# A router input transposed by DMA and sine arguments summed in PSUM, in a kernel of a long convolution and a gated MLP

## The chip, the cores and the metric

The kernel runs on one core of one Trainium2 chip. Its time is the device time of one execution in microseconds (us). Five engines work side by side: TensorE (PE in the profile; its weight loads are PEld), VectorE (DVE), ScalarE (ACT), GpSimd (POOL) and SyncE (SP, which here only issues DMAs). Every engine executes its own list of instructions strictly in order, and lists wait for each other by semaphores.

## The reference

The input `x` has 2048 tokens of 512 channels. Two results are mixed by a gate per token.

```
g = sigmoid((x * gate_w).sum(-1))
# a: a state space layer, as a long causal convolution over the tokens
dt = exp(log_dt);  P[d,n,l] = exp(dt*(A_re + 1j*A_im)*l)           # 512 channels, 128 states, 2048 lags
K  = einsum("dn,dnl,dn->dl", Cc, P, dt*Bc).real                    # one filter per channel
a  = causal convolution of x with K (by FFT in the reference) + x * Dskip
# b: a gated MLP for the two tokens with the largest score, added to x
r = x @ w_r;  idx = top 2 of r
b = x;  b[idx] += sigmoid(r[idx]) * ((silu(x[idx] @ w_gate) * (x[idx] @ w_up)) @ w_down)
out = g * a + (1 - g) * b
```

Both `g` and `r` need, for each token, a product of the 512 channels with a vector. On TensorE that takes `x` with the channels on the partitions, the transpose of how `x` lies in memory.

## The kernel before

**Filters.** `P` is a product of exponentials and of sines and cosines of angles that grow with the lag. A lag is split into a coarse and a fine part: table 1 (`tab1`) holds the complex exponentials for the coarse lags, table 2 (`tab2`) for the fine ones, already multiplied by `C` and `B`. Each is made twice, for the two halves h = 0 and 1 of the channels. `kgen(h)` multiplies the tables on TensorE (L920) and sorts the filter into rows with small selecting matmuls (L933 to L949); `kspec(h)` turns it into its spectrum with the constant matrices `c_ksp` in the tiles KP (L975).

**Angles.** `B16` holds dt times A_im in units of 1/65536 of a turn, rounded to within one turn, in f32. For a group of up to four multiples, `trig` (L652) scales `B16` by each multiple into an int32 tile (`SCL`, ACT or DVE, L477), takes the Sin of the low 16 bits (L665), adds a quarter turn to the whole group (L667) and takes the Sin again for the cosine (L669). Table 1 uses three such groups for each half (four, four and two multiples, and the rest by doubling); table 2 uses two.

**Convolution.** `forward(blk)` transforms the two blocks of 1024 tokens with the matrices `c_fwd` in the tiles F (L896, groups of four matmuls), its results are evicted into `X` (L901), and four DMAs from GpSimd accumulate halves of it (L906). `products(h)` multiplies spectra on DVE, `inverse(h)` transforms back on TensorE (L1057), and the result is gated and stored.

**Routing.** `routing` (L759) makes the transposed input XT with 64 TensorE transposes of 128x128 in eight groups (L766), each evicted from PSUM by one copy of 128x1024 (L769, helper `EV`, L467). The matmuls of L781 give the two scores of each token. A chain of small DVE operations finds the two best tokens (four turns over TensorE, L800). Then `gat` (L828) gathers the two tokens, the MLP's first matmuls follow (L849, with the loads WG and WU of `w_gate` and `w_up`), its last ones (L863, here called dn, with the loads WD0 and WD1), a transpose of the result (L870), and a scaling into the row tile ZB on DVE (L873, called zby below). ZB also holds the row Dskip, loaded by a DMA of its own (zbd, L580), and zby waits for that load. An indirect DMA from GpSimd (L874) then adds the two rows to `out`, where two DMAs, dx0 and dx1 (L879), have copied the input before; `reload` (L883) reads it back into U.

**Order.** The order of all instructions on all engines, including the DMA queues, is written out in the text `ORDER`, which engine does an eviction or a scaling in `SECOND`, and which PSUM bank or place a temporary tile has in `PLACES`. SP therefore issues its DMAs in a fixed order as well, and a DMA whose wait isn't met holds up those behind it. WD lies where XT lay, so its loads wait for L781; the four tiles KP0 to KP3 lie where F lay, so their loads wait for the last forward matmuls that read each F.

Of the kernel before, what the change touches and what calls it, by code (L numbers as in the profile page):

```python
# [10 lines left out]
F32 = mybir.dt.float32  # L11
I32 = mybir.dt.int32
I16 = mybir.dt.int16
# [340 lines left out]
def small_mats():  # L354
# [17 lines left out]
    "00k00500201601501l00000100300700d00h00i00400900600800u00g00e00c00j00f00n00l00m08e00o00p00q00s00r00t01g01d01e01h00x00y00z01c01801704003x04104801a01b03z"  # L372
    "04a03y01003v02502604900w00v01x01v01101208g04b01w01r01z04201y02002302402102701t05g01u04504301s02202804c01304604402902a02j02k05h03w02l02m02n01402o06k06j"
    "04d05i02p04e04705m05j02q02r05k05n01q04f02s03401o01p02b01j01m01i01902c01n01f02t06s02u03702v06r04i02w02x02y03802z06p03004j03103204l03303904k03c04g04m03d"
    "04h03i06l03a03504n06m08f04o03g03b06q06n06o04p03j04q05o04r03h02d04u04s03m06x06y04t06z07002e01k04w07107204y03n04v08i06t08j04z04x06u07300a03l07403k03o00b"
    "03p05007607505p08l05405305q06v06w05l07807706703q06605108v07907a08k05r05u05t05207c08m03r08s06808n08t03s03603t07d07b08u05507i07h07g07f07e07l07k06906a05v"
    "07j05905a05605b05c05x08w08h06b08x05d05708z08o05e05w05y08y08p09009t09v07m07p07n07o07q08q09o08r09107r09309n07s07t09207v02g09407u09p09w09509602h09709807z"
    "07y09q09u08107w09r09s0a10a20a308207x09x09y06c06d06005z0a40a50a60a80a70aa0a906e09z08c0a00ac0ab0ad0ae06g06f06108a06208d06308009a09905806h08308409b06402f"
    "08509e08603e09g03f0af08708b0ag0ai09c0aq0ah05s03u05f06506i09d0am09i09f0ar0b00b209j0880b10as0an0ak0aj0b30al0at0b70b80b90b40b50b60ax0ay0au0av09h09k0ap0ao"
    "09l09m0az0ba0be02i0c50890cd0bd0bb0bg0bh0aw0c60cc0c70c30c20c10bc0bk0bj0c00bi0bf0bl0dk0bm0bn0bp0bo0bq0dl0dh0bt0bu0br0bs0by0di0ce0c80bv0bw0cf0bx0d30d40cg"  # L380
    "0ct0c90c40ch0co0ca0dd0dg0bz0cv0cu0df0de0d50dj0ci0cb0cw0d00et0cj0dn0d60cq0cx0cp0d10d20do0dt0cy0cz0cl0eu0ck0d70du0da0dr0dp0dm0dq0d80dx0cr0d90e80db0dc0cm"
    "0cn0f30f40dv0ey0ez0dw0cs0ds0e40e70ea0ev0ew0e90ef0e30eb0ed0eh0el0ex0fs0f00fv0f50f10e50fo0e60fu0fr0fn0em0f70f60f20ec0eg0en0ee0ej0ft0fw0fx0fz0f80eo0g00g5"
    "0ek0ei0f90gh0fq0fp0fy0g30gi0fa0fb0fc0fd0g10ge0gd0g60gj0g70gl0dy0gf0gg0gk0gn0g80fe0gm0go0gq0g20g40dz0gp0ff0fg0fi0gr0fh0fj0h00gv0fm0fl0gw0gx0gy0fk0es0gs"
    "0gt0gu0er0ep0eq0e00gb0ga0gc0e20g90h10e10h90gz0ha0h40h50h60h20h70hb0h30h80hc"
)
SECOND = (
    "000000000000000000000000000000000000100000000000000000000000000000101010100010100000100100000000000000000000000000100010000000000000000000000010010001"
    "000110010100001010010010011010000000000000000000000000000000000000000000000000000000001010010010100000100000000000000000000000000000000000000000000000"
    "000001000001010000000100000110100000100100000000101000000010000010000000000000000000000000000000000000000000000000000000000000000000000000000000000000"
    "000000000000000000000000000000000000000000000000000000000000000000000000000000000000000000000000000000000000000000000000000000000000000000000000000000"  # L390
    "0000000000010011000100000"
)
PLACES = (
    "2406154064740000000020660011001266446040110064604014001100111016606022026424242200101026264262451016541026000171234265"
)
KB = 1024


def bass_gated_mix__ssm_conv_s4__moe_arch_mod__prompt_kernel(nc, A_u, A_A_re, A_A_im, A_B_re, A_B_im, A_C_re, A_C_im, A_log_dt, A_Dskip,
# [20 lines left out]
    kp_c = const(kspec_mats(), "c_ksp")  # L420

    with ExitStack() as es:
# [76 lines left out]
        KP = [B("kp%d" % i, oF + 4 * i * KB, 4 * KB) for i in range(NU)]  # L499
        X = B("x", oX, 32 * KB)  # L500
# [7 lines left out]
        TMP = [B("tmp%d" % i, oTI[0] + (8 + 2 * i) * KB, 2 * KB, F32) for i in range(3)]  # L508
        CM1 = B("cm1", oTI[1], 4 * KB, F32); CM2 = B("cm2", oTI[1] + 4 * KB, 4 * KB, F32)
# [70 lines left out]
        DQ([(ZB(64, 1, 0, (1, D)), dr(A_Dskip, 0, (D, 1), (1, D)))], [], [(ZB, "d")], 1024)  # L580
        DQ([(WG(0, 128, 0, (NF, 4), (1, NF)), dr(B_w_gate, 0, (NF, 128), (128 * NF, 4), (1, NF)))], [], [WG], 1835008)
# [39 lines left out]
        STT(f512(B16), f512(tb_), c16, f512(TMP[2]), ALU.mult, ALU.subtract, [tb_, TMP[2]], [B16])  # L621
        c2 = lambda b, c=0: b(0, 128, c, (D, 2), (1, D))
# [29 lines left out]
        def trig(h, angs, ts, wide, tag, nn=None):  # L652
# [17 lines left out]
            return s  # L670
        def tab1(h, ts):
# [87 lines left out]
        def routing():  # L759
            for q in range(8):  # L760
                bb = misc(True)
                def tr(h, q=q, bb=bb):
                    last = None
                    for t_ in range(2):
                        for db in range(4):
                            last = h.transpose(bb(0, 128, db * 256 + t_ * 128, (1, 128)), U(0, 128, (2 * q + t_) * D + db * 128, (1, 128)), IDN(0, (1, 128)))  # L766
                    return last
                P.op(PE, tr, uk(2 * q, 2 * q + 1) + [CBI], [bb], cost=0.455)
                EV(XT[0](0, 128, q * 256, (2 * L, 2), (L, 2), (1, 256)), bb(0, 128, 0, (512, 2), (256, 2), (1, 256)), [bb], [(XT[i], q) for i in range(4)])  # L769
# [383 lines left out]
```

## Time and profile before

The runs of the kernel before took 153.70, 153.71 and 154.03 us, with a median of 153.71 us. The profiled execution took 153.72 us; its span, from the first to the last instruction, was 151.9 us, so 1.8 us lie outside the span.

| | busy us | share of the span | instructions |
|---|---|---|---|
| PE (matmuls) | 129.7 | 85% | 1605 |
| PEld (weight loads) | 96.4 | 63% | 1613 |
| DVE | 138.2 | 91% | 199 |
| ACT | 131.1 | 86% | 218 |
| POOL | 24.8 | 16% | 17 |

A window of the profile gives, for a stretch of the span, the busy time and the number of instructions of each engine, the clock granted to TensorE (1.00 is full), the busy share of the 16 DMA engines and the rate. A row of a group gives the line, the engine, the operation, the shapes and the count, then the busy time of all and the mean of one, then the idle time before them and what ended it. A mean of one on DVE and ACT is from start to end; back to back, the next one starts some 0.1 us before that end, so five copies of 0.69 us each take 3.0 us together.

### The profile page before, as it was taken

How to read it: one execution, taken by the hardware profiler on the slowest of the kernel's cores; microseconds unless marked ns; L12 is line 12 of the kernel's file. 1: busy time of each engine (PE TensorE's matmuls, PEld its weight loads, DVE VectorE, ACT ScalarE, POOL GpSimd, SP SyncE). 2: the span in 40 equal slices, each digit the busy share in tenths (PEclk: the TensorE clock that was granted, in tenths of full speed). 3: DMA queues.
4: the chain of work that ended last, by engine and by line, in shares of the span. 5: the costliest groups of instructions: out<-in, count | busy, mean ns of one | idle time of the engine just before them, and what ended most of it. 6: DMA issues, size and time to landing. Idle time of an engine off the chain costs nothing.

```text
span 151.9 us, 3786 instructions
## 1 busy us (share of the span) xinstructions
PE 129.7 (85%) x1605; PEld 96.4 (63%) x1613; DVE 138.2 (91%) x199; ACT 131.1 (86%) x218; POOL 24.8 (16%) x17
## 2 busy tenths in 40 slices
PE   0974787467989986979996999997999999999990
PEld 0944542464354336973454787995888867888880
DVE  0499999999999999999999974999999999999961
ACT  3599999999999999999999569397599999999731
POOL 3000001000122999910055000001000000000000
PEclk9999999955699999999997799999999999999999
DMA  5999999939908604000389997006800001014154
GB/s 136 344 293 388 414 403 404 350 108 330 365 2 119 162 0 138 4 5 0 92 231 254 275 275 118 6 4 203 356 0 2 4 2 35 0 54 123 35 173 138
DMA packets 14546, 24.09 MB, mean 159 GB/s; under 512 B 1175, under 2 KB 10146, under 8 KB 14370
## 3 DMA queue, kind: packets, MB, share of 16 engines
q1 hardware_dynamic: 11410, 21.11, 40.8%
q0 software_dynamic: 2144, 2.10, 9.0%
q10 hardware_dynamic: 976, 0.66, 1.6%
q8 instruction: 12, 0.20, 0.5%
q14 instruction: 4, 0.03, 0.1%
HBM read 19.66 MB, written 4.20 MB: 157 GB/s over the span
## 4 chain that ended last, share of the span: by engine, by line
PE 53%; DVE 28%; ACT 8%; DMA 6%; issue 3%; SPq 0%; ACTq 0%
PE ps L1057 18%; DVE AR L452 18%; PE ps L975 13%; PE ps L920 11%; DMA AR<-c_ksp 4%; DVE AR L467 3%; ACT AR L463 3%; PE ps L896 2%; PE ps L1010 2%; DVE AR L477 2%; ACT AR L467 2%; ACT AR L667 2%; DMA AR<-c_bf 2%; DVE AR L456 1%; PE ps L933 1%
## 5 line engine op out<-in xcount | busy, mean ns | idle before, releaser
L452 DVE TENSOR_TENSOR AR<-AR 128x1024 bf16<-128x1024 bf16 (+8 forms) x129 | 115.6, 952 | 7.2 <-DMA AR<-c_bf 3.8
L467 ACT ACTIVATE AR<-ps 128x1024 bf16<-128x1024 f32 (+10 forms) x45 | 35.0, 807 | 9.1 <-PE ps L975 4.7
L896 PE MATMUL ps<-AR 128*128 128x512 bf16 x122 | 31.0, 405 | 3.2 <-ACT AR L901 1.5
L1057 PE MATMUL ps<-AR 128*128 128x256 bf16 x256 | 29.5, 273 | 0.0
L1057 PEld LDWEIGHTS ps<-AR 128*128 128x128 bf16 x256 | 25.0, 98 | 3.1
L896 PEld LDWEIGHTS ps<-AR 128*128 128x128 bf16 x128 | 12.5, 104 | 18.9 <-issue 3.6
L975 PE MATMUL ps<-AR 128*128 128x256 bf16 x160 | 20.8, 288 | 1.3 <-DMA AR<-c_ksp 1.3
L975 PEld LDWEIGHTS ps<-AR 128*128 128x128 bf16 x160 | 16.4, 103 | 5.3 <-DMA AR<-c_ksp 1.6
L920 PE MATMUL ps<-AR 128*128 128x84 bf16 (+1 forms) x512 | 17.9, 196 | 1.7 <-DVE AR L452 1.7
L920 PEld LDWEIGHTS ps<-AR 128*128 128x128 bf16 x512 | 17.8, 96 | 2.2 <-ACT AR L463 2.2
L463 ACT ACTIVATE AR<-AR 128x1024 bf16<-128x1024 int16 (+5 forms) x24 | 18.5, 773 | 0.5 <-DVE AR L477 0.3
L463 ACT ACTIVATE ps<-AR 128x256 f32<-128x256 bf16 (+1 forms) x36 | 18.0, 549 | 0.1
L874 POOL DMA_INDIRECT out_dram<-AR x1 | 16.2, 16210 | 2.8 <-ACT AR L477 2.8
L901 ACT ACTIVATE AR<-ps 128x1024 bf16<-128x1024 f32 x16 | 15.9, 1015 | 0.0
L1068 ACT ACTIVATE AR<-ps,AR 128x256 bf16<-128x256 f32 x28 | 11.4, 482 | 4.3 <-PE ps L1057 3.4
L477 ACT ACTIVATE AR<-AR 128x256 int32<-128x256 f32 (+2 forms) x28 | 13.8, 518 | 0.0
L463 ACT ACTIVATE AR<-ps 128x512 bf16<-128x512 f32 (+1 forms) x18 | 11.9, 757 | 2.0 <-PE ps L597 2.0
L906 POOL DMA_DIRECT2D AR<-AR x4 | 5.3, 1464 | 17.6 <-ACT AR L901 16.0
L667 ACT ACTIVATE AR<-AR 128x1024 int32<-128x1024 int32 (+1 forms) x9 | 7.8, 867 | 0.1
L766 PE MATMUL ps<-AR 128*128 128x128 bf16 x64 | 4.6, 220 | 3.2 <-DVE AR L452 1.4
L477 DVE TENSOR_SCALAR AR<-AR 128x256 int32<-128x256 f32 (+2 forms) x20 | 6.5, 336 | 0.0
L766 PEld LDWEIGHTS ps<-AR 128*128 128x128 bf16 x64 | 3.6, 98 | 4.3 <-DVE AR L467 2.0
(67 smaller groups left out, 91.3 us busy)
## 6 DMA issues: line engine op xcount, KB each, us to landing
AR<-c_ksp SPq DMA_DIRECT2D x5, 512.0 KB, 3.9
AR<-in_A_u_dram SPq DMA_DIRECT2D x4, 512.0 KB, 5.5
AR<-c_fwd SPq DMA_DIRECT2D x4, 512.0 KB, 7.9
AR<-AR POOLq DMA_DIRECT2D x4, 512.0 KB, 12.9
AR<-out_dram SPq DMA_DIRECT2D x4, 512.0 KB, 10.1
AR<-c_inv SPq DMA_DIRECT2D x1, 2048.0 KB, 8.8
AR<-in_B_w_up_dram SPq DMA_DIRECT2D x1, 1792.0 KB, 12.0
AR<-in_B_w_gate_dram SPq DMA_DIRECT2D x1, 1792.0 KB, 16.1
```

Of the source, the lines that this page charges most:

```text
L452: return P.op(DVE, lambda h: h.tensor_tensor(out=o, in0=a, in1=b, op=op), rd, wr, cost=cst or tt_cost(o, a, b), **k)
L463: return P.op(ACT, lambda h: h.activation(out=o, in_=a, func=func, scale=scale, bias=bias), rd, wr, cost=0.185 + nel(o) * 0.833e-3 + (0.09 ...
L467: return P.op((ACT, DVE), (lambda h: h.activation(out=o, in_=a, func=ACTF.Copy), lambda h: h.tensor_copy(o, a)), rd, wr, cost=(0.185 + n * ...
L477: return P.op((ACT, DVE), (lambda h: h.activation(out=o, in_=a, func=ACTF.Copy, scale=c), lambda h: h.tensor_scalar(out=o, in0=a, scalar1= ...
L667: P.op((DVE, ACT), (lambda hh: hh.tensor_scalar(out=w, in0=w, scalar1=16384.0, scalar2=None, op0=ALU.add), lambda hh: hh.activation(out=w, ...
L874: P.op(POOL, lambda h: h.indirect_dma_start(dr(out, 0, (D, L), (1, D)), bass.IndirectOffsetOnAxis(ap=IDX(0, 2, 0, (1, 1)), axis=0), ZB(0, ...
L896: last = h.matmul(pb(0, 128, part * 512, (1, 512)), F[ft](0, 128, ((par * 4 + st) * 2 + part) * 128, (1, 128)), U(0, 128, (blk * 8 + st * ...
L901: P.op((ACT, DVE), (lambda hh, o=o, i_=i_, sc=sc: hh.activation(out=o, in_=i_, func=ACTF.Copy, scale=sc), lambda hh, o=o, i_=i_, sc=sc: hh ...
L920: last = hh.matmul(pb(0, 128, g // 6 * 512 + g % 6 * W4 + o, (1, n)), TP[h][1 - i // 2](0, 128, (b0 + g) * 128, (1, 128)), r[i](0, 128, (b ...
L975: last = hh.matmul(pb(0, 128, n * 256, (1, 256)), KP[u](0, 128, tau * 128, (1, 128)), KC[h](0, 128, jg * 256, (1, 256)), start=(k == 0 and ...
L1057: r = hh.matmul(pb(0, 128, e * 256, (1, 256)), G(0, 128, ((par * 2 + part) * 4 + ft) * 512 + (2 * t2 + e) * 128, (1, 128)), X(0, 128, blk ...
L1068: r = hh.activation(out=U(0, 128, tb * D + h * HC, (1, HC)), in_=pb(0, 128, e * 256, (1, HC)), func=ACTF.Copy, scale=SG(0, 128, 64 + tb, ( ...
```

## The change

The change has three parts.

- **Router input.** The eight groups of transposes and their eight evictions are gone. Four DMAs on SP's queue load the transposed input straight from memory, one for each 128 channels, all 2048 tokens, with `transpose=True`. The columns of XT are now in the order of the tokens, so L781's matmuls read them with a step of 2. `X` and all else of the routing are as before.
- **Angles of table 1.** From A_im and dt, six operations (five of them on 128x512 elements) make a value with few bits, split in two bf16 parts, PA[0] and PA[1]. For each group of table 1, `angles` takes the place of `trig`: TensorE multiplies the parts with a constant matrix `c_ang` (tile AN, a DMA of 164352 bytes) that holds the multiples, and sums them in PSUM on top of a large constant, so that the low 16 bits are the angle; ACT takes the Sin straight from PSUM; a matmul with a constant adds a quarter turn; ACT takes the Sin again. Table 2 keeps `trig`.
- **Order.** `ORDER`, `SECOND` and `PLACES` are new. Among others, SP issues XT1, XT0, XT3 and XT2 among the first loads; the loads of `c_bf`'s second part (cbo) and of zbd come after dx1 and before dx0; KP4 and two of the accumulating DMAs come later. `tab1(1)` is built ahead of the last load of KP instead of after it, which changes only its numbering.

```
+def angle_mats():   # 128 x 642: for each group the multiples, then 1.5 * 2**23 and 16384
...
+        AN = B("an", oF + 16 * KB, 2 * 642)
+        PA = [B("pa%d" % i, oF + 16 * KB + 1536 + i * KB, 1 * KB) for i in range(2)]
...
+        DQ([(AN(0, 128, 0, (1, 642)), an_c[:, :])], [], [AN], 164352)
...
+        for db in range(4):
+            P.op(SP, lambda h, db=db: [h.dma_start(XT[db](0, 128, 0, (1, L)), dr(A_u, db * 128, (D, L), (1, 128)), transpose=True)], [], [XT[db]], cost=0.5, nbytes=786432, dma=True)
...
+        TS(DTC(0, 128, 0, (1, 4)), DTP(0, 128, 0, (1, 4)), -8.0 * c16, ALU.mult, [DTP], [DTC])
+        TT(XR[0](0, 128, 0, (128, 4), (1, 128)), PRM(0, 128, D, (128, 4), (1, 128)), DTC(0, 128, 0, (1, 4), (0, 128)), ALU.mult, [(PRM, 1), DTC], [XR[0]])
+        TS(f512(XR[1]), f512(XR[0]), MG, ALU.add, [XR[0]], [XR[1]])
+        STT(f512(XR[2]), f512(XR[1]), MG, f512(XR[0]), ALU.subtract, ALU.subtract, [XR[0], XR[1]], [XR[2]])
+        EV(f512(PA[0]), f512(XR[2]), [XR[2]], [PA[0]])
+        TT(f512(PA[1]), f512(XR[2]), f512(PA[0]), ALU.subtract, [XR[2], PA[0]], [PA[1]])
...
+        def angles(h, g, ts):
...
+            def add(hh, col, first):
+                for b in range(nb_):
+                    r = hh.matmul(pb(0, 128, b * 512, (1, w)), IDN(0, (1, 128)), AN(0, 128, col, (0, w)), start=first, stop=False, skip_group_check=True)
+                return r
+            def ang(hh):
+                add(hh, 640, True)
+                for x in range(2):
+                    for k in range(4):
+                        for b in range(nb_):
+                            r = hh.matmul(pb(0, 128, b * 512 + k, (4, w // 4)), PA[x](64 * h, 64, k * 128, (1, 128)), AN(64 * h, 64, c0 + b * (w // 4), (1, w // 4)),
+                                          start=False, stop=False, skip_group_check=True)
+                return r
...
+            P.op(PE, ang, [CBI, AN, *PA], [pb], cost=nb_ * (0.2157 + 8 * 0.1))
+            AC(so(0), lo, ACTF.Sin, [pb], [(s, "s")], scale=SC16, tset=ts)
+            P.op(PE, lambda hh: add(hh, 641, False), [CBI, AN], [pb], cost=nb_ * 0.2157)
+            AC(so(2), lo, ACTF.Sin, [pb], [(s, "c")], scale=SC16, tset=ts)
...
-                s = made[g] = trig(h, ANG1[4 * g:4 * g + j0], ts[g // 2], True, "1%d%d" % (h, g), 4) if j0 else place("snc", TRG, oI + 8 * KB, 6 * KB)
+                s = made[g] = angles(h, g, ts[g // 2]) if j0 else place("snc", TRG, oI + 8 * KB, 6 * KB)
...
-            for q in range(8):
-                bb = misc(True)
...
-                P.op(PE, tr, uk(2 * q, 2 * q + 1) + [CBI], [bb], cost=0.455)
-                EV(XT[0](0, 128, q * 256, (2 * L, 2), (L, 2), (1, 256)), bb(0, 128, 0, (512, 2), (256, 2), (1, 256)), [bb], [(XT[i], q) for i in range(4)])
...
-                                last = h.matmul(b(0, 128, tb * 2, (1, 2)), XT[db](0, 128, tb * 128, (1, 128)), WL(0, 128, db, (4, 2)), start=(db == 0), stop=(db == 3))
+                                last = h.matmul(b(0, 128, tb * 2, (1, 2)), XT[db](0, 128, j * 1024 + st * 256 + par, (2, 128)), WL(0, 128, db, (4, 2)), start=(db == 0), stop=(db == 3))
...
         for u in range(NU):
+            if u == NU - 1:
+                tab1(1, (1, 1))
             DMA([(KP[u](0, 128, 0, (1, 2048)), kp_c[:, u * 2048:(u + 1) * 2048])], [], [KP[u]], 524288)
-        tab1(1, (1, 1))
```

Besides these lines, `ORDER`, `SECOND` and `PLACES` are replaced as a whole.

More of the change, by code (lines that the diff above doesn't have):

```diff
@@ L371 @@
 ORDER = (
[L372 to L383, printed above, removed]
@@ L395 @@
 )
 KB = 1024
+def angle_mats():
+    out = np.zeros((128, 642))
+    c = 0
+    for g in range(4):
+        j0 = DBL1.get(g, (4, 0, 0, 0))[0]
+        ts = [a // 8 for a in ANG1[4 * g:4 * g + j0]]
+        for i, t in enumerate(ts):
+            for p in range(128):
+                out[p, c + p % 64 * j0 + i] = t
+        c += 64 * j0
+    out[:, 640], out[:, 641] = 1.5 * 2.0 ** 23, 16384.0
+    return out
 def bass_gated_mix__ssm_conv_s4__moe_arch_mod__prompt_kernel(nc, A_u, A_A_re, A_A_im, A_B_re, A_B_im, A_C_re, A_C_im, A_log_dt, A_Dskip,
@@ L508, in bass_gated_mix__ssm_conv_s4__moe_arch_mod__prompt_kernel @@
         TMP = [B("tmp%d" % i, oTI[0] + (8 + 2 * i) * KB, 2 * KB, F32) for i in range(3)]
+        XR = [B("xr%d" % i, oTI[1] + (8 + 2 * i) * KB, 2 * KB, F32) for i in range(3)]
+        DTC = B("dtc", oTI[0] + 6 * KB + 64, 32, F32)
         CM1 = B("cm1", oTI[1], 4 * KB, F32); CM2 = B("cm2", oTI[1] + 4 * KB, 4 * KB, F32)
@@ L759, in routing @@
         def routing():
-            for q in range(8):
-                bb = misc(True)
[L762 to L767, printed above, removed]
-                P.op(PE, tr, uk(2 * q, 2 * q + 1) + [CBI], [bb], cost=0.455)
-                EV(XT[0](0, 128, q * 256, (2 * L, 2), (L, 2), (1, 256)), bb(0, 128, 0, (512, 2), (256, 2), (1, 256)), [bb], [(XT[i], q) for i in range(4)])
             w8 = misc(True)
```

38 lines of the change are left out of this document (31 added, 7 removed).

## The prediction

> **What bounds the kernel now.** I read the page first, for who is full and when.
>
> ```profile
> span 151.9 us, 3786 instructions
> ...
> DVE  0499999999999999999999974999999999999961
> ACT  3599999999999999999999569397599999999731
> ...
> PEclk9999999955699999999997799999999999999999
> DMA  5999999939908604000389997006800001014154
> ...
> PE 53%; DVE 28%; ACT 8%; DMA 6%; issue 3%; SPq 0%; ACTq 0%
> ```
>
> DVE and ACT are full from slice 3 on, the DMA engines in the first 30 us, and PE carries half of the chain. Two dips stand out: the granted clock near 80 us, and DVE near 90 us. Next the chain in order of time, to see who hands over to whom.
>
> ```profile
> 50.44 7.76 DVE AR L452 x7
> ...
> 58.33 8.96 PE ps L920 x256
> ...
> 75.47 6.10 DMA AR<-c_ksp
> 81.57 0.05 issue
> 81.61 8.83 PE ps L975 x64
> ...
> 107.22 7.09 PE ps L975 x64
> ```
>
> DVE works up to 58.2 us without a break; then `kgen(0)` starts, and from there the end hangs on PE. At 81.6 us PE waits for the last KP load. The same 64 matmuls then take 8.83 us, against 7.09 at 107 us. Last, windows by stage.
>
> ```profile
> 58.00:75.00 17.00, 15.67 (x286) 11.73 (x288) 16.79 (x30) 16.90 (x26) 7.20 (x1) 1.00 0.11 34
> 75.00:82.00 7.00, 5.66 (x71) 3.21 (x69) 7.00 (x8) 6.95 (x11) 3.93 (x3) 1.00 0.94 245
> 81.60:93.60 12.00, 11.93 (x86) 9.35 (x88) 9.08 (x13) 9.03 (x12) 0.43 (x2) 0.86 1.10 247
> 123.00:148.00 25.00, 24.95 (x215) 20.82 (x214) 23.84 (x30) 21.50 (x51) 0.00 (x0) 1.00 0.22 64
> ```
>
> Columns are PE, PEld, DVE, ACT, POOL, clock, DMA share and rate. PE is full from 81.6 to 148, so what moves the end is when `kspec(0)` starts and at which clock, and when DVE can start the products (93.19 us here, after 2.9 us of waiting for an accumulating DMA).
>
> **The change, part by part.** Times are of the profiled execution (153.72 us, of which 1.8 outside the span, equal to the median).
>
> ```profile
> L467 DVE COPY AR<-ps 128x1024 bf16<-128x1024 bf16 x6 | 3.8, 687 | 0.0
> L766 PE MATMUL ps<-AR 128*128 128x128 bf16 x64 | 4.6, 220 | 3.2 <-DVE AR L452 1.4 <-DVE AR L467 1.3 <-DVE AR L459 0.4
> L477 ACT ACTIVATE AR<-AR 128x256 int32<-128x256 f32 x23 | 9.1, 420 | 0.0
> ```
>
> *DVE.* Gone before 58 us: six XT copies at 0.6 back to back (3.6), five scalings at 0.2 (1.0), one quarter turn (0.6). Moved to ACT: one square (0.6), one scaling (0.2). Added: the six operations on XR and PA; one is tiny, one goes to ACT, four cost 0.6, 0.35, 0.6 and 0.6 (rows of L452, L456 and L459 at 512 elements), in all 2.3 with the tiny one. Moved on: 0.9 of small ones. Sum: 2.8 us less before `kgen(0)`, and the new operations fill the 2.0 us in which DVE waited at 4.5 us for the scaled A_im. Nothing is bought by that alone, unless what DVE waits for also comes earlier.
>
> *ACT.* Gone: 15 scalings at 0.31 (4.6), five quarter turns (3.9), two XT copies (1.8); PA[0] adds 0.6. ACT is full in the windows from 58 to 82 us, so evictions there can come up to a microsecond earlier; elsewhere it has room. The Sin reads PSUM in place of SBUF; I take the same 0.95 us for 1024 elements (f32 evictions from PSUM and Sins from SBUF stand within 0.03 of each other).
>
> *PE.* Gone: 64 transposes, 0.45 for each eight (3.6). Added: 100 matmuls, of which 20 are 512 wide (0.22 each, L896) and 80 are 128 wide with a spread output (0.1 each, L597): 12.4 us, 6 for each half. Half 0 lies before 20 us, where PE had idle time; of half 1, 4 us lie between the MLP's first matmuls and dn, where PE waits for WD0 anyway (below), and 1.0 us lies right ahead of `kgen(0)`, on the path.
>
> *DMA.* Added are 2.1 MB of XT and 0.16 MB of AN, in a stretch where all 16 engines are full; KP4 (1.3 us) and cbo (0.4) leave it. The rows that XT reads are 256 bytes long. The trace's packets of 256 bytes take a median of 18 ns, those of 4096 bytes 159 ns. So 8192 rows over 16 engines cost 9.2 us, 2.3 a load. The bounds: 1.27 a load, 5.1 in all, if a transposing load runs like `c_fwd`'s 4096-byte rows; and 3.4 a load, 13.7 in all, like the accumulating DMAs (9.0% of 16 engines' span for four of 0.5 MB), which also work on the data on its way. I take 2.3, since the row length is given by the code and is nearest. The Trainium skill ("DMA: Bandwidth & Descriptors", Latency and other measured facts) gives 261 GB/s for a transposing DMA with non-contiguous rows; an estimate from it is 8.0 us in all, which would make the sum below about 1 us shorter. No row of before shows a transposing load.
>
> Now the queue, by landings in the trace. Before, the last of u, F2, F3, cbo and the parameters landed at 15.6 us. Now the last of u, with F2, F1, XT and AN, lands 0.1 + 9.2 later, 24.9 (XT itself at about 18, and L781 ran at 18.1 before: a microsecond of DVE at most). The MLP's loads follow with the spacing they had (4.5, 5.2, 2.3, 2.75): WD0 at 39.7 instead of 32.9, then F3 and F0 (1.3 each) at 42.3. SP waits with dx1 for WD0. A dx took 5.5 us (32.95 to 38.49), so dx1 lands at 45.3, and cbo and zbd, queued behind it, at about 46. **zby waits for zbd** in the new place. DVE, gapless, would be there at 3.8 + 36.6 + 1.8 (sum of its operations and small waits) = 42.2; it waits till 46.2 (before: 47.5), and the tables behind it in DVE's list wait too. So does PE: the bank of the transposed row comes free with zby, then 13 forward groups at 0.87 to 0.9 (20 matmuls in 4.49) and the 1.0 of angles follow. `kgen(0)` starts at 46.6 + 11.5 + 1.0 = 59.1, against 58.3: the gain of DVE is gone in the queue, and 0.8 more.
>
> *From there to the end.* `kgen(0)` 9.0, quarter turns 0.2, a gap of 0.7, eight forward groups 7.1: last one done at 76.1 (75.0 before). Selecting took 4.6 (75.4 to 80.0), so PE is ready at 80.7. The last KP is issued at 76.1; it took 6.1 us before, beside two earlier KP loads' rest, the reload and an accumulating DMA. Now both accumulating DMAs of the first block start after the zeroing of table 1's half 1 on POOL's list, at about 67, and are through by 76, so KP takes about what such a load takes at the median (3.9): 80.0. PE doesn't wait, keeps its clock, and `kspec(0)` takes 12.0 - 1.7 = 10.3 (64 matmuls at 7.1): `kgen(1)` starts at 91.0, not 93.64. That is 2.6 us gained. DVE has 42.85 + 0.7 from zby to the products: 90.0; the third accumulating DMA, with one fewer (3.4 us) in the jam, lands at 90 to 91 instead of 93.1. Products start 2.6 earlier too. Both then have the work they had (DVE 53.1 against 52.9, PE equal), so the span is 149.3 and the time **151.1**.
>
> **Rivals.**
> *Transposing loads are slow.* Place: SP's queue ahead of the MLP's loads. At 3.4 a load all landings above are 4.5 later, `kgen(0)` starts at 63.6 and `kgen(1)` at 95.5: 1.9 slower than before, 155.6. It decides from 2.95 a load on, where the 2.6 are used up; each further microsecond a load costs four. For it: nothing in the trace shows a better rate for 256-byte rows than mine, and XT is in the queue ahead of everything. Against: 2.3 already has the short rows in it. The Trainium skill ("VectorE: DVE Perf Modes", The three transpose paths and the rules behind it) speaks against the change: 1309 ns for a 128x128 block by DMA, 390 by TensorE, which it prefers wherever PSUM will do; the trace's 56 ns a block, pipelined, makes the gap wider still. Chance 0.35.
> *The clock dip stays.* If the last KP lands as late after its issue as before (6.1) PE waits 1.5 us, the clock falls again, and only the products' and ACT's share remains: 152.9. For it: the reload is issued right behind. Chance 0.15.
> *Loads at plain speed* (1.27): zbd lands at 42, zby at 43, bound by PE; `kgen(0)` starts at 56, and the end comes 5 earlier: 148.5. Against: the 18 ns. Chance 0.12.
> *No change.* The 0.8 lost at `kgen(0)` and what is gained at KP cancel: 153.7. Chance 0.08.
> The forecast keeps 0.30.
>
> **Numbers.** A measurement of this kernel can tell about 0.2%, 0.3 us. Faster are the forecast, the dip and the plain loads: 0.57. The range takes in the plain loads (with 0.5 below) and the slow ones up to 3.6 us each; beyond that I leave out about 0.15.
>
> **What would show it.** Right: XT landings 2 to 2.5 us apart at about 18 us; WD0 at 40; zby on DVE after an idle stretch of some 4 us that ends with the zbd load; `kgen(0)` at 58 to 60; no c_ksp piece in the chain, the clock 1.00 from 76 to 94, products from about 90.5. Wrong: SP busy for microseconds with one XT issue, L781 later than 20 us with DVE idle, or `kgen(0)` later than 62; on the other side, zby before 44 us.

## The result, and the profile after

The changed kernel took 160.56 us (median of 158.18, 159.96, 161.16 and 163.54), the kernel before 153.7: a ratio of 1.036, with a 95% interval of 1.024 to 1.048. The change makes the kernel some 5.5 us slower by the ratio and 6.9 by the medians; forecast were 151.1 us, and the forecast's range took in transposing loads of up to 3.6 us each, which by its own sum is some 156 us. The four runs differ by TensorE's clock (mean granted clock 0.945, 0.934, 0.913 and 0.894, in the order of their times), the ratio rests on the two at the higher clocks, and the profiled execution is the one of 163.54 us, so the times read off below are at the upper end.

The page of the changed kernel: the span, the busy tenths, and the shares of the chain.

```profile
span 161.7 us, 3837 instructions
...
DVE  0899287999794099998999999999999999999971
ACT  3595499698863477989897747976679999999621
...
PEclk9996555799555599999999999999999999999999
DMA  5999999999990000043489999400860000002356
...
PE 80%; DMA 6%; ACT 6%; SPq 4%; issue 2%; DVE 0%
```

DVE was 28% of the chain and is 0% now; PE was 53% and is 80%. The dip of the clock at 80 us is gone, as forecast. But where the clock before was at half once in the first 60 us, from 31 to 41 us, it is so twice now, from 13 to 30 us and from 40 to 57, and DVE has a hole from 50 to 57 us.

The groups of the angle sums (L718: the narrow matmuls of `angles`; L711: the constants):

```profile
L718 PE MATMUL ps<-AR 64*128 64x128 bf16 x80 | 16.6, 456 | 0.4 <-issue 0.4
...
L711 PE MATMUL ps<-AR 128*128 128x512 bf16 x14 | 6.8, 558 | 2.3 <-DMA AR<-c_ang 1.5
```

The two rows are 23.4 us of PE where 12.4 were forecast, and the second shows only 14 of the 20 constants. The chain in order of time shows where:

```profile
42.48 3.52 PE ps L718 x16
...
46.98 3.52 PE ps L718 x16
50.50 1.60 PE ps L909 x56
...
70.95 5.04 PE ps L966 x144
...
86.98 5.59 DMA AR<-c_ksp
92.61 5.41 PE ps L1021 x48
...
103.32 8.35 PE ps L966 x240
```

L909 is dn, L966 `kgen`, L1021 `kspec` (L863, L920 and L975 before). dn comes right behind two large sums of half 1, at 50.43 us instead of 42.95, and `kgen(0)` at 70.87 instead of 58.30. From there to `kgen(1)` (103.32) it is 32.4 us, against 35.3 before: those 2.9 us were won. The windows from 40 to 56 us show at what clock PE worked (columns as before: PE, PEld, DVE, ACT, POOL, clock, DMA share, rate):

```profile
40.00:44.00 4.00, 3.04 (x38) 2.36 (x36) 3.07 (x8) 3.88 (x7) 0.00 (x0) 0.54 1.26 462
44.00:48.00 4.00, 4.00 (x18) 2.75 (x17) 3.93 (x11) 1.96 (x3) 0.00 (x0) 0.50 1.05 399
48.00:52.00 4.00, 4.00 (x68) 3.59 (x68) 2.14 (x2) 1.95 (x2) 0.00 (x0) 0.50 0.01 2
52.00:56.00 4.00, 3.76 (x13) 1.26 (x11) 0.00 (x0) 2.00 (x6) 0.00 (x0) 0.50 0.01 4
```

From 44 to 52 us PE is listed busy without a gap and has half its clock all the same. A narrow matmul takes 0.22 us there (3.52 for 16); the eight of the small group at 69.97 us, at full clock, take 0.98 together. Between the end of the MLP's first matmuls (41.6) and dn (50.4) the two large sums and their constants take 8.8 us.

### The profile page after: what moved, and what is told of

Same layout as the page of the kernel before. It is cut to its first block, busy times and chain, and to the rows that moved or that the text cites. A ratio compares the mean times of both kernels' runs of the same rounds, so it can differ in the third digit from the quotient of the medians.

```text
span 161.7 us, 3837 instructions
## 1 busy us (share of the span) xinstructions
PE 148.1 (92%) x1638; PEld 109.1 (67%) x1649; DVE 138.5 (86%) x195; ACT 121.7 (75%) x194; POOL 20.0 (12%) x17
## 4 chain that ended last, share of the span: by engine, by line
PE 80%; DMA 6%; ACT 6%; SPq 4%; issue 2%; DVE 0%
PE ps L942 18%; PE ps L1103 17%; PE ps L1021 11%; PE ps L966 11%; PE ps L718 10%; DMA AR<-c_ksp 3%; PE ps L711 3%; DMA AR<-c_ang 2%; ACT AR L478 2%; PE ps L1056 2%; SPq L495 2%; SPq L602 2%; PE ps L895 2%; PE ps L979 1%; ACT AR L947 1%
## 5 line engine op out<-in xcount | busy, mean ns | idle before, releaser
L482 ACT ACTIVATE AR<-ps 128x1024 bf16<-128x1024 f32 (+8 forms) x41 | 32.2, 806 | 11.2 <-PE ps L1021 4.6
L942 PE MATMUL ps<-AR 128*128 128x512 bf16 x125 | 32.3, 413 | 0.7 <-ACT AR L947 0.4
L478 ACT ACTIVATE AR<-ps 128x512 bf16<-128x512 f32 (+3 forms) x30 | 22.7, 801 | 12.2 <-PE ps L718 6.2
L1103 PEld LDWEIGHTS ps<-AR 128*128 128x128 bf16 x256 | 25.1, 98 | 3.0
L942 PEld LDWEIGHTS ps<-AR 128*128 128x128 bf16 x128 | 13.3, 106 | 17.0 <-issue 4.1
L1021 PE MATMUL ps<-AR 128*128 128x256 bf16 x160 | 19.0, 273 | 1.1 <-DMA AR<-c_ksp 1.1
L1021 PEld LDWEIGHTS ps<-AR 128*128 128x128 bf16 x160 | 15.4, 98 | 4.2 <-DMA AR<-c_ksp 1.4
L966 PEld LDWEIGHTS ps<-AR 128*128 128x128 bf16 x512 | 17.8, 96 | 0.5 <-ACT AR L947 0.2
L966 PE MATMUL ps<-AR 128*128 128x84 bf16 (+1 forms) x512 | 18.0, 196 | 0.1
L718 PE MATMUL ps<-AR 64*128 64x128 bf16 x80 | 16.6, 456 | 0.4 <-issue 0.4
L718 PEld LDWEIGHTS ps<-AR 64*128 64x128 bf16 x80 | 13.9, 194 | 3.8 <-issue 3.8
L920 POOL DMA_INDIRECT out_dram<-AR x1 | 11.9, 11893 | 21.3 <-DVE AR L471 21.3
L711 PE MATMUL ps<-AR 128*128 128x512 bf16 x14 | 6.8, 558 | 2.3 <-DMA AR<-c_ang 1.5
L492 DVE TENSOR_SCALAR AR<-AR 128x1024 bf16<-128x1024 bf16 (+2 forms) x15 | 5.2, 350 | 4.2 <-ACT AR L478 3.4
L492 ACT ACTIVATE AR<-AR 128x256 int32<-128x256 f32 (+1 forms) x13 | 8.3, 659 | 0.4 <-DVE AR L467 0.4
L478 ACT ACTIVATE AR<-AR 128x512 bf16<-128x512 int16 (+5 forms) x12 | 7.5, 630 | 1.2 <-DVE AR L751 0.8
```

Of the source, the lines that this page charges most:

```text
L478: return P.op(ACT, lambda h: h.activation(out=o, in_=a, func=func, scale=scale, bias=bias), rd, wr, cost=0.185 + nel(o) * 0.833e-3 + (0.09 ...
L482: return P.op((ACT, DVE), (lambda h: h.activation(out=o, in_=a, func=ACTF.Copy), lambda h: h.tensor_copy(o, a)), rd, wr, cost=(0.185 + n * ...
L492: return P.op((ACT, DVE), (lambda h: h.activation(out=o, in_=a, func=ACTF.Copy, scale=c), lambda h: h.tensor_scalar(out=o, in0=a, scalar1= ...
L711: r = hh.matmul(pb(0, 128, b * 512, (1, w)), IDN(0, (1, 128)), AN(0, 128, col, (0, w)), start=first, stop=False, skip_group_check=True)
L718: r = hh.matmul(pb(0, 128, b * 512 + k, (4, w // 4)), PA[x](64 * h, 64, k * 128, (1, 128)), AN(64 * h, 64, c0 + b * (w // 4), (1, w // 4)) ...
L920: P.op(POOL, lambda h: h.indirect_dma_start(dr(out, 0, (D, L), (1, D)), bass.IndirectOffsetOnAxis(ap=IDX(0, 2, 0, (1, 1)), axis=0), ZB(0, ...
```

## The experiments

Three theories stood: A, the angle sums on PE (their place ahead of the logits and dn, and the half clock); B, the transposing loads, which delay all loads behind them; C, the new order. "Logits" is the start of L827 (L781 before), and hb3, in the expectations, is the product of the MLP's two hidden vectors on DVE, which dn reads. All of a row but the median and the ratio is from one profiled execution, in us; for e13, e16 and e19 no ratio can be given. e3 and e11 leave out the transposing, so their router reads other values, and e2's angles are other ones: these three are prices, not kernels to use.

| run | median | ratio [95%] | logits | WD0 landed | dn | `zby` | `kgen(0)` |
|---|---|---|---|---|---|---|---|
| before | 153.7 | 1 | 18.1 | 32.9 | 42.95 | 47.5 | 58.3 |
| changed | 160.56 | 1.036 [1.024, 1.048] | 21.7 | 42.3 | 50.4 | 57.0 | 70.9 |
| e1 dn first | 163.27 | 1.058 [1.051, 1.065] | 18.3 | 42.4 | 43.3 | 56.4 | 69.4 |
| e7 dn first, mended | 163.76 | 1.057 [1.047, 1.068] | 17.7 | 41.2 | 41.7 | 47.0 | 69.4 |
| e2 128 rows | 156.38 | 1.011 [1.006, 1.016] | 18.4 | 41.9 | 45.3 | 49.6 | 62.9 |
| e6 128 rows, half zero | 157.45 | 1.017 [1.011, 1.023] | 18.9 | 42.5 | 45.7 | 50.0 | 63.3 |
| e8 256 columns | 156.18 | 1.012 [1.004, 1.020] | 18.0 | 41.8 | 43.7 | 49.5 | 62.7 |
| e10 128 rows, 256 columns | 155.1 | 1.004 [1.002, 1.007] | 19.6 | 42.9 | 44.0 | 49.0 | 61.4 |
| e12 e10, other order | 154.26 | 1.000 [0.997, 1.004] | 19.5 | 43.3 | 44.8 | 50.6 | 63.0 |
| e3 plain XT | 159.9 | 1.035 [1.028, 1.042] | 17.8 | 36.2 | 46.7 | 53.2 | 67.2 |
| e11 e10, plain XT | 151.25 | 0.975 [0.966, 0.984] | 17.6 | 36.0 | 40.3 | 44.6 | 57.5 |
| e4 loads alone | 163.09 | 1.052 [1.045, 1.060] | 25.9 | 44.9 | 52.2 | 56.8 | 67.6 |
| e9 loads alone, logits first | 166.72 | 1.076 [1.070, 1.082] | 16.6 | 44.2 | 47.9 | 52.5 | 68.6 |
| e13 angles alone | 171.9 | | 28.5 | 39.5 | 56.4 | 62.0 | 75.7 |
| e16 the same, other layout | 164.89 | | 30.5 | 41.6 | 58.6 | 64.3 | 78.0 |
| e19 the same, third layout | 164.12 | | 26.0 | 37.2 | 55.3 | 61.9 | 76.0 |
| e15 angles alone, sums as e10 | 157.45 | 1.018 [1.013, 1.023] | 23.5 | 34.0 | 46.1 | 51.7 | 64.0 |
| e18 the same, other layout | 158.36 | 1.025 [1.018, 1.031] | 23.0 | 33.6 | 46.0 | 51.8 | 64.1 |
| e14 half of XT by loads | 157.04 | 1.012 [1.006, 1.019] | 24.3 | 37.8 | 45.9 | 51.8 | 64.6 |
| e17 the same, other layout | 154.64 | 0.998 [0.994, 1.002] | 20.1 | 37.6 | 43.0 | 48.7 | 61.1 |

**Order (e1, e7).** Only `ORDER` and `PLACES` differ from the changed kernel:

```
PE then: ... 119, sums(1) x2, dn, add, fwd 171, fwd 172, L916, ...
PE e1:   ... 119, dn, fwd 171, fwd 172, L916, sums(1) x2, ...
PE e7:   ... 119, dn, fwd 171, L916, fwd 172, sums(1) x2, ...; on ACT rtsrs ahead of the Sins, on DVE zby ahead of 252
```

> The changed kernel with another order alone: half 1's two large angle sums (L711, with the Sins and quarter turns that follow them) stand on PE's list behind dn (L909), two forward groups and the transposed row (L916) instead of ahead of dn. Theory A (the angles' matmuls cost the time: 4.1 us each at a clock of 0.50, ahead of what DVE waits for): dn starts when hb3 is there, at 45.6 instead of 50.4, zby at about 51 instead of 57.0; but the angle sums then stand between zby and the 13 forward groups and PE has hardly any idle time from 41 us on, so kgen(0) comes at 67 to 70 instead of 70.9 and the time is 157 to 160. Theory B (the transposing loads): zby follows the loads (zbd at 48) and the 13 forward groups follow zby, kgen(0) at about 61, time about 152. Theory C (the new order, of which this undoes one piece): 3 us or more off at kgen(0) without the PE work changing.

> The changed kernel with another order alone: dn (L909) and the transposed row (L916) ahead of half 1's two large angle sums on PE, and the two small things that zby also needs (the scale rtsrs of L868 on ACT, zby itself on DVE) ahead of what follows from the angles. In the first try of this, rtsrs stood behind the angles' Sins on ACT and zby came at 56.4 all the same. Theory A: zby at about 49 instead of 57.0, bound by the zbd load; PE has the same work from 41 us on with the waits of about 3.5 us gone, so kgen(0) at 66 to 68 and the time 157 to 159. Theory B: the order of PE's list does nothing for loads, 160. Theory C (the new order costs the time): zby 8 us earlier gives kgen(0) back, at 62 or earlier, time below 155.

All three theories missed the time, which is 2 points above the changed kernel's in both runs; of the expected `kgen(0)` only A's of e1 (67 to 70) held. `zby` came 10 us earlier in e7, and `kgen(0)` came only 1.5 us earlier. The waits of DVE in e1, and in e7 (a line each; what waited, for what, us in all, times, longest):

```profile
DVE AR L471 <- ACT AR L482: 8.5, 1, 8.5
```

```profile
DVE AR L467 <- ACT AR L492: 7.8, 1, 7.8
```

ACT's list held the Sins of half 1 ahead of a small scale (rtsrs, e1) and of the scaling nb0 (e7) that DVE's table needs. With the sums moved back, ACT stood before those Sins for 8 us, and DVE behind ACT. So these two orders of PE's list moved the wait into ACT's list and on to DVE.

**Rows (e2, e6).**

```diff
-  PA[x](64 * h, 64, k * 128, (1, 128)), AN(64 * h, 64, ...)
+  PA[x](0, 128, k * 128, (1, 128)), AN(0, 128, ...)      # e6: AN twice as wide, with zeros in the other half's rows
```

> The changed kernel with the angle matmuls over 128 rows of PA and AN instead of the 64 of one half: the same number of matmuls, the same 128 columns and the same places in PSUM; the angles are then sums over both halves, so the values that the tables hold are other ones. It asks whether it is the 64 rows that keep the granted clock at 0.50 while PE is listed busy. If they do: the clock in 44 to 56 us goes to 1.00, half 1's two large sums take about 2.2 us each instead of 4.1, the first two forward groups 0.75 instead of 1.43, and by theory A kgen(0) comes at 64 to 66 instead of 70.9 and the time is about 154 to 156. If they don't, clock and times stay as they were (160). Theory B: the clock may rise, but kgen(0) still follows the loads and the time moves by less than 2 us.

> The changed kernel with the angle matmuls over all 128 rows and the right sums: the matrix AN is twice as wide, with zeros in the rows of the other half (its load grows from 164 to 328 KB, and PA stands in other memory). Theory A (64-row matmuls keep the clock at half, and the angles' time on PE delays zby and kgen(0)): as in the 128-row run before it, where the time was 156.4: clock near 1.00 from 44 us on, kgen(0) at 62 to 65, time 155 to 158. If it is not the rows that an instruction names but the data in them that counts (half of them are zero here), the clock stays at 0.50 and the time at 159 to 161. Theory B (loads): 160 or 0.4 us more.

The windows of e2, in which half 1's sums begin at 38.4 us, and behind them one of e3 (plain loads, below), where sums over 64 rows run from 38 to 46.7 us:

```profile
40.00:42.00 2.00, 2.00 (x12) 2.00 (x10) 1.93 (x5) 0.91 (x2) 0.00 (x0) 0.50 1.05 397
42.00:44.00 2.00, 2.00 (x10) 1.45 (x9) 2.00 (x5) 1.15 (x2) 0.00 (x0) 0.52 1.67 588
44.00:46.00 2.00, 2.00 (x38) 2.00 (x37) 1.97 (x5) 1.74 (x2) 0.00 (x0) 1.00 0.17 66
```

```profile
44.00:46.00 2.00, 2.00 (x11) 2.00 (x10) 2.00 (x2) 1.14 (x2) 0.00 (x0) 0.50 0.00 0
```

Over 128 rows the clock is back 5.5 us after the sums begin, and `kgen(0)` comes 8 us earlier. With zeros in half of the rows (e6) it is back at 44.5, 5.9 us after they begin. Over 64 rows it stayed at 0.50 through 8.6 us of sums and beyond, in the changed kernel and in e3, and in e13, e16 and e19 below as well; over 128 rows it was back 2.8 to 5.9 us after the sums began in all eight traces whose sums met the half clock (e2, e6, e10, e11, e12, e15, e17, e18). So the rows that the instruction names count, whatever lies in them. A held, with e2's time 0.4 us above its range and its `kgen(0)` a microsecond ahead of it, and e6 within both; B's (under 2 us) fell.

**Fewer and wider (e8), and both (e10, e12).**

```diff
-  for b in range(nb_): matmul(pb(0, 128, b * 512 + k, (4, w // 4)), PA..., AN(..., c0 + b * (w // 4), (1, w // 4)))
+  matmul(pb(0, 128, k * (n // 4), (1, n // 4)), PA..., AN(..., c0, (1, n // 4)))      # the Sin reads four blocks
```

> The changed kernel with fewer and wider angle matmuls: each stationary block of PA serves both banks in one matmul of 256 columns (128 for the small group), so 40 narrow matmuls in place of 80, still over 64 rows; the Sin reads PSUM through another access pattern (four blocks instead of one run). Theory A: at a clock of 0.50 a large sum takes about 2.6 us (8 matmuls at 0.27 and 2 at 0.22) instead of 4.1, so PE has 6 us less in all, kgen(0) at 66 to 68 and the time 156 to 158. Theory B: PE's work doesn't matter, 159 to 161. Should the Sins from four blocks take longer than 1.03 us, ACT loses that much eight times.

> The changed kernel with both mends of the angle matmuls, otherwise in its own order: 128 rows (zeros for the other half) and one matmul of 256 columns for both banks. The runs before had 157.5 with the first alone and 156.2 with the second. Theory A (angles on PE at half clock): half 1's large sums at 2.4 us cold, the clock back at 1.00 by 44 us, the first two forward groups at 0.75 instead of 1.43, kgen(0) at 60 to 62, time 154 to 156. Theory B (after that mending the loads are the bound): kgen(0) stays where it was, at 62.7, and the time at 156 to 157.

> The run e10 with another order in three places: the transposed row (L916) and rtsrs ahead of the second forward group behind dn, zby behind two additions of the table on DVE's list, and two steps of the router (L846) ahead of the forward groups that wait for u and F2. In the run e8 DVE waited 2.6 us for L916 and 1.9 for L846. Theory A: PE is full from 38 us on, so DVE's 4 us buy only what PE's list gives, kgen(0) at 59 to 61, time 153 to 155. Theory C (waits in the new order cost the time): DVE's time counts in full, kgen(0) at 57 to 58, time 151 to 152.

The group of e10 that answers to L718 above:

```profile
L718 PE MATMUL ps<-AR 128*128 128x256 bf16 x32 | 5.9, 346 | 0.0
...
L718 PE MATMUL ps<-AR 128*128 128x128 bf16 x16 | 1.7, 266 | 0.0
```

7.6 us instead of 16.6. A large sum takes 2.5 us at half clock, 1.3 at full (start to start). Two things changed in the narrow matmuls, their number and where their output goes. At full clock a matmul of 128 columns whose output goes to every fourth element takes 0.11 us from start to start (the small group, at 70 us in the changed kernel), one of 256 columns side by side the same 0.11 (e10, at 12.4 us), and one of 128 side by side 0.056 (e10, at 61.1 us): the spread output had doubled the price. In e8 the clock came back at 48.3 us, behind the first forward groups, so `kgen(0)` gained more than A expected. Each mend alone brings 1.9 to 2.5 points of the ratio, both together 3.1 of the 3.6. The new order of e12 comes 0.4 points lower still (the intervals overlap) and is level with before. A held for all three times; `kgen(0)` came earlier than it expected in e8 and later in e12.

**The loads (e3, e11).**

```diff
-  h.dma_start(XT[db](0, 128, 0, (1, L)), dr(A_u, db * 128, (D, L), (1, 128)), transpose=True)
+  h.dma_start(XT[db](0, 128, 0, (1, L)), dr(A_u, db * 128 * L, (L, 128), (1, L)))
```

> The changed kernel with the four XT loads as plain loads of the same 512 KB each, 128 rows of 4096 bytes, not transposed: the router gets other inputs and chooses another expert row. It prices the transposing. Theory B (transposing loads cost the time): XT landings 1.3 us apart instead of 2, SP free at once, WD0 at about 37 instead of 42.3, kgen(0) below 62, time at or below 153. Theory A: the MLP's weights and with them L895 come 4 to 5 us earlier, but half 1's angles still stand ahead of dn at half clock: zby at about 52, kgen(0) at about 66, time 156 to 158, so slower than before all the same.

> The run e10 with the four XT loads plain (4096-byte rows, the same bytes, not transposed): the router gets other inputs. With PE's extra time mostly gone it asks again what the transposing costs; in the changed kernel itself (run e3) landings 6 us earlier moved the time by nothing, 159.9 against 160.6. Theory B: now the MLP's weights are what PE and DVE wait for, so 5 us of them come back: dn at about 39, kgen(0) at 56 to 58, time 149 to 152. Theory A: PE's 15 forward groups behind F0 are full anyway and the time falls by 1 to 2 us against e10 at most, to 153 to 155.

The windows of e10 and of e11 while XT is loaded:

```profile
12.00:16.00 4.00, 3.02 (x22) 1.99 (x23) 3.96 (x7) 3.62 (x5) 0.31 (x1) 1.00 1.11 198
```

```profile
12.00:16.00 4.00, 1.58 (x12) 0.86 (x10) 3.96 (x7) 3.97 (x5) 0.31 (x1) 0.97 1.04 411
```

The DMA engines are full in both, but transposing they move 198 GB/s, plain 411. The load of WU lands at 32.5 us in the changed kernel and 26.3 in e3, at 32.95 and 26.3 in e10 and e11: transposing costs 6.1 to 6.6 us for the four loads. (Each window holds other loads too; in e11 the last XT load landed at 14.05 us.) In e3 that bought next to nothing (1.035 for 1.036): dn waited for the end of the sums (46.7), while hb3 was there at 41.7 and WD0 at 36.2. In e11 it bought 3.9 us: dn ran at 40.3, right behind hb3 (40.0) and the last matmul of the sums (started at 40.3). In e3 B missed, and A was right about the sums ahead of dn but 2 us below the time; in e11 B held and A fell. Two chains meet at dn, and only the later one can be shortened with effect.

**The loads alone (e4, e9).** Before's kernel and order, with the transposes and copies out and the four XT loads put ahead of u on SP; in e9 also the logits and the router's four small matmuls ahead of the forward groups on PE.

> The kernel before with the transposing loads alone: the eight blocks of TensorE transposes and their copies are gone, the four XT loads stand on SP ahead of u, F2 and the MLP's weights; the angles are scaled as before and the order is before's otherwise. Theory A: WD0 lands about 9 us later than before's 32.9, at about 42, just when dn started before (42.95), so the loads cost little: kgen(0) at 58 to 60 and the time 152 to 155. Theory B: everything behind the loads is 9 us late as in the changed kernel, kgen(0) at 66 or later, time 158 to 161. Theory C (the order costs the time): no loss here, 150 to 153.

> The kernel before with the transposing loads alone, as in the run e4, with one thing mended: there L781 (the router's logits) stood behind a forward group on PE that waited for F2, and ran at 25.9 us instead of 18; here the logits and four small steps of the router stand ahead of the forward groups. Theory A: the loads cost little, since WD0 had 10 us to spare before dn: logits at 18 to 19, dn at 45 to 47, kgen(0) at 57 to 60, time 151 to 155. Theory B (9 us of loads ahead of everything): the MLP's weights are what waits, WU and WG at 33 and 37 and WD0 at 45, dn not before 48, zby not before 52, kgen(0) at 63 or later, time 157 to 160.

Both ratios lie above the changed kernel's, in e4 with intervals that overlap a little. In e4 the logits stood behind a forward group that waits for F2 (24.5 us). In e9 they ran at 16.6, but SP's list holds F1 and dx1 behind dx0, which waits for WD0: F1 landed at 52.0 instead of 41.2, dx1 at 55.9 instead of 43.8. In this window PE had nothing to do:

```profile
52.00:56.00 4.00, 0.39 (x5) 0.20 (x4) 3.47 (x4) 0.04 (x1) 0.00 (x0) 0.97 0.72 116
```

A's reason, that WD0 had 10 us to spare, was true of dn and false of the queue behind WD0. B came nearest: its `kgen(0)` held in both, its times were 2 and 7 us too low. C expected no loss in the order of before and fell. That the new order is what lets the kernel bear the loads is an inference: e10 and e12 bear them in it, but no run has the loads alone in the new order.

**The angles alone (e13, e16, e19; with the mended sums e15, e18).** The changed kernel without XT loads; the transposes of before are back among its first 20 us, in three layouts.

> The changed kernel without the transposing loads: the eight blocks of TensorE transposes and their copies (five on DVE, three on ACT) are back, between the angle sums of half 0, u is loaded ahead of F2 and F1, and all else is as in the changed kernel, 64-row angle sums included. Theory B (loads): every load lands 8 us or more earlier, WD0 at about 33, kgen(0) at 58 or earlier, time 153 or less. Theory A (angles): the large sums of half 1 stay ahead of dn at half clock, 4.1 us each, and half 0's compete with the transposes: kgen(0) at 63 to 66, time 156 to 160, so still slower than before without a single byte more to load but AN.

> The change's angle part alone as it was written (64 rows, 80 narrow matmuls), in the changed kernel's order, without XT loads, the transposes placed as in e15. Theory A: half 1's large sums still stand ahead of dn for 8 us at half clock whatever the loads do, kgen(0) at 62 to 66, time 156 to 159. Theory B: with 9 us of loads gone kgen(0) is back at 58 and the time at 153 to 155.

> The run e16 (the change's angle part alone, 64 rows and 80 narrow matmuls as it was written, no XT loads) with the first 20 us laid out as in e18 and the rest in the changed kernel's order. It is e18 with the sums as the change has them (and without its three moves at L916 and zby). Theory A: half 1's large sums stand ahead of dn at half clock for 8 us and the first forward groups behind them at 1.43: kgen(0) at 62 to 66, 4 to 7 us later than in e18, time 156 to 160, and so the angles alone cost most of the 7 us. Theory B: within 2 us of e18.

> The run e10 with no XT loads at all: eight blocks of eight transposes on TensorE ahead of and between half 0's angle sums, five copies on DVE and three on ACT, with more places in PSUM for them than in the run e13; u, F2 and F1 are loaded right behind AN; L916, rtsrs and zby stand as in e12. It is the change's angle part alone, with its matmuls mended. Theory B: WD0 lands at 33 or 34, but DVE now has 3 us of copies more and no waits to take them from, so kgen(0) at 56 to 59 and the time 149 to 154. Theory A: 153 to 155.

> The run e15 (mended sums, no XT loads) with its first 20 us laid out anew in the same way; there the logits ran at 23.5. Five copies on DVE and three on ACT remain. Theory B: logits at 18 to 19, dn at 39 to 42, kgen(0) at 56 to 59, time 150 to 154; it is better or worse than the half-and-half kernel by the 2 us of further copies against the 4 us of loads, as far as DVE or the router's chain is what waits. Theory A: 153 to 155.

None answers B cleanly. With the loads gone WD0 lands up to 9 us earlier, but transposes, copies and half 0's sums now want PE, PSUM and DVE in the same 10 us, and the logits come at 23 to 30 us instead of 18. In the median all five took longer than either theory expected. In e13 one PSUM place served five of the eight blocks, one after the other. From the logits to the MLP's first matmul it is 13.7 to 15.7 us in these five (13.7 before, 14.2 in e18), so what the loads gave, the router took. e19 against e18 is near A's 4 to 7 us in the medians (164.1 and 158.4), but that is not shown: e19's runs spread from 159.0 at a clock of 0.952 to 168.4 at 0.883, and the one at 0.952 lies within a microsecond of e18, as B expected (e16's one at 0.947, 162.2, lies 4.7 us above e15). With 64 rows the time goes with the clock that a run had.

**Half of it (e14, e17).** e10 with two of the four blocks of XT by loads and two by TensorE.

> The run e10 (angle sums over 128 rows and 256 columns) with half of the transposing loads: two of the four 128-column blocks of the router's input come by the XT loads, the other two by TensorE (four blocks of eight transposes, copied three times on DVE and once on ACT), u is loaded ahead of the two XT loads; L916, rtsrs and zby stand as in e12. Theory B in the form that the runs e10 and e11 left (behind the angles, the next bound is the 4 us by which transposing loads are longer than plain ones of the same bytes): WD0 lands at about 37 instead of 43, kgen(0) at 57 to 58, DVE pays 2 us of copies out of its 5 us of waits, time 150 to 153. Theory A alone (PE's list is all that counts): nothing gained against e12, 154 to 155.

> The run e14 (mended sums, half of the router's input by XT loads, half by TensorE) with its first 20 us laid out anew: there the logits ran at 24.3 us, because the transposes stood behind the angle sums and a single copy on ACT, and the loads' 5 us were lost again in the router. Here the transposes go ahead, over four places in PSUM, with one copy on ACT right behind the first Sin. Theory B (behind the sums the transposing loads bound it): logits at 18 to 19.5, dn at 41 to 42, kgen(0) at 57 to 59, time 151 to 153.5, below before. Theory A (PE's list): 154 to 155.

e14 lost time ahead of the router's logits in the same way, and was slower than both theories expected. e17 has them at 20.1 and WD0 at 37.6, and is level with the kernel before: 0.998, from 0.994 to 1.002. It is within A's range and has the lowest ratio of the kernels that transpose the router's input by loads in part or whole, but e12's 1.000 lies in its interval; neither the times of theory B (150 to 153 us for e14, 151 to 153.5 for e17) nor a kernel faster than before was reached.

## Why the prediction was wrong

**The step that failed** is the sum of PE: "Added: 100 matmuls ... 12.4 us, 6 for each half ... of half 1, 4 us lie between the MLP's first matmuls and dn, where PE waits for WD0 anyway". Three things in it were wrong. The size: 23.4 us, since 0.1 us for a narrow matmul was a price at full clock and most of them ran at half (0.22); the two large sums of half 1 took 8.8 us, not 4. e10 shows 3.1 of the 3.6 points to be the shape of these matmuls, their rows and their output together. The cover: the loads had moved the MLP's first matmuls themselves (the last ended at 41.6, before at 34.9), and hb3 was there at 45.5, WD0 at 42.3, so 3.9 us of waiting were left to be filled, where before it was 8.0 (34.9 to 42.95); the sums' last matmul started at 50.0. And what stands behind in PE's order: in half 1 dn and the first two forward groups, at 1.71 us each instead of 0.87; in half 0 the logits (XT had landed at 18.5, they ran at 21.7). The text set a limit for being wrong, logits later than 20 us with DVE idle and `kgen(0)` later than 62, and both happened. But the logits' delay belongs to this one execution: the clock fell at 13.0 us, within half 0's first sum, while in e1 and e7, with the same list up to there, it was at 1.00 then and the logits ran at 18.3 and 17.7. That half 1's sums ahead of dn meet the half clock is in all five traces that have these sums ahead of dn (the changed kernel, e3, e13, e16, e19).

**The queue.** XT landed at 18.5 (forecast about 18), its last three loads 2 us apart; that step was right. Behind it every landing was 2.4 to 2.6 us later than forecast: WD0 42.3 (39.7), F0 44.8 (42.3), dx1 47.7 (45.3). SP was held for 2.0 to 3.3 us by each transposing issue (the first from 2.59 to 5.84 us, where a plain one so early takes 0.4 to 0.5) and issued cf, u and F2 only from 16 us on. The plain loads of the same bytes show 6.1 to 6.6 us of transposing, 1.3 + 1.6 = 2.9 us a load as the queue behind feels it: between the 2.3 taken and the 3.4 of the slow rival, at the 2.95 from which that rival was to decide. By the prediction's own sum, 2.9 a load makes 153.5 us, level with before, and within half a percent of level is where e10 and e12 are, with the sums mended. As far as these numbers go, this term ate the gain, and the sums made the loss. Against plain loads its price was 3.9 us (e10 and e11); in the changed kernel it lay under the sums. The Trainium skill ("DMA: Bandwidth & Descriptors", Latency and other measured facts) gives 261 GB/s for such loads. The last three landed 2.00 and 2.07 us apart for 512 KB each, which is 262 and 253 GB/s and agrees; in e10 it was 2.6 and 2.1 us, 202 and 248 GB/s.

**zby** did not wait for zbd (about 48 us) but for PE's transposed row (56.3); in e7, where dn stood ahead of the sums, the wait for zbd was the last one, as the prediction had it (`zby` at 47.0 for 46.2). **DVE and ACT**: ACT's busy time fell by 9.4 us (131.1 to 121.7; forecast 9.7, or 8.9 with the square and the scaling that it took over), so that term was right. It bought nothing, DVE being idle for 6.9 us ahead of zby and 3.4 for half 0's Sins.

**From `kgen(0)` on** the steps held: 32.4 us to `kgen(1)` for 31.9 forecast, 13 forward groups in 11.1 for 11.5, the clock at 1.00, `kspec(0)` in 10.7 for 10.3. The KP load took 5.6 us, not 3.9, so a c_ksp piece is in the chain, against the sign named; PE waited only 1.1 for it. The clock's dip did not stay; its window now:

```profile
92.60:103.30 10.70, 10.64 (x88) 8.36 (x90) 10.64 (x11) 7.27 (x9) 2.05 (x2) 1.00 1.05 258
```

**Left open.** What the angle part alone costs in a layout that has the logits at 18 us (three were tried), and why the clock is at half in one run and full in the next at the same place: half 0's first two sums took 2.9 and 4.1 us in the changed kernel and 2.1 to 2.2 each in e1, e3 and e7 (first start to last start), with the same instructions. The traces show one thing about it: within each of them the clock changed only at times that lie 3.41 us or a multiple of it apart (in e12 at 12.72, 16.14, 22.96, 29.79, 36.62 and 43.45 us), and these times lie elsewhere in every run. The place of the sums ahead of the forward groups with ACT's list rearranged as well was not tried.

## What to carry to other kernels

Price a new matmul at the clock of the place where it will stand, and look at its rows and its output: here a stretch of matmuls over half of the rows was listed as full and yet did not bring the clock up, and an output spread over every fourth element doubled the price. Before an idle stretch is spent as cover, ask whether the same change moves its ends; here the loads moved the MLP's first matmuls into the gap that the sums were to fill. When two parts of a change delay two chains that meet at one instruction, undoing one part can show nothing, as in e3: mend the other one first.

## What the runs showed of the hardware

- Matmuls over 64 rows and 128 columns, back to back, did not bring the clock up from 0.50 in 8.6 us (the changed kernel, e3, e13, e16, e19); over 128 rows it came up after 2.8 to 5.9 us (eight traces), also with zeros in half of them (e6, 5.9). Already up, it stayed at 1.00 through two such 64-row sums from 49 to 53.7 us in e1; in e7 it came up 2.1 us into them, at 50.2, right behind forward groups over 128 rows. The Trainium skill ("TensorE: Matmul & The Clock Gate", Part 1: The HAM clock gate) lets the full clock come after some 3.4 us of sustained activity, whatever the number of matmuls; the traces agree for 128 rows, and not for 64.
- A transposing load of 512 KB held SP for 2.0 to 3.3 us in the changed kernel, and four of them cost the loads behind them 6.1 to 6.6 us more than plain ones of the same bytes, at 198 against 411 GB/s in the windows shown.
- At full clock a matmul of 128 columns with its output in every fourth element takes 0.11 us from start to start, as long as one of 256 columns side by side; 128 side by side take 0.056 (e10). With both the spread and half of the matmuls gone, a large sum takes 1.3 us instead of 2.4 (e10 against e7).
